# Fewer unread products, a re-searched plan, and the last rows cast in two operations, in a two-layer transformer kernel

## Chip, cores and metric

The kernel runs on one core of one Trainium2 chip. The metric is the device time of one execution in microseconds (us), read as the median of several executions. Nothing but this kernel runs on the core.

## What is computed

Two transformer layers over x of 2048 rows by 448 columns, in bfloat16, with the same weights in both layers. Each layer is a layernorm, attention with 16 heads of 28 columns, and a dense part of 448 to 1792 to 448 columns with a squared ReLU:

```python
x = x + _A_ref(_layernorm(x), A_wqkv, A_wo)         # softmax(q k^T / sqrt(28)) v, then wo
x = x + _B_ref(_layernorm(x), B_w1, B_b1, B_w2, B_b2)   # h = relu(x w1 + b1); (h * h) w2 + b2
x = x + _A_ref(_layernorm(x), A_wqkv, A_wo)
x = x + _B_ref(_layernorm(x), B_w1, B_b1, B_w2, B_b2)
```

The scores are 2 layers x 16 heads x 2048 x 2048, 134 million exponentials. They are the bulk of the work of every engine but SyncE.

## The kernel before

**Units.** A layer's rows are cut into blocks of 256 query rows, and the last 256 rows of layer 1 into two blocks of 128. A pass is one block and one group of four heads. Its work is cut into units of 128 x 512 scores, one bank of PSUM each; there are 2048 units in all. TensorE (PE) makes the scores of a unit with 32-row products (line 1107, `sc<-Q_sb,K_sb`), three units at a time into a tile of three banks, of which there are two (`ps_sc`).

**Exponentials.** ScalarE (ACT) takes the exponential of the two or three banks of a tile in one instruction (line 1139, `pts<-sc`, 1024 or 1536 columns). Some units, here 328 of 2048, are kept from ACT: VectorE (DVE) copies their scores away (line 1211), GpSimd (POOL) and DVE make the exponential out of integer and float arithmetic on the bits (lines 1236, 1242, 1251, 1263), or DVE closes it alone with a longer operation (line 1275). Such a unit has a bank of its own (`mt`) or the third bank of a tile. PE then multiplies by the values (line 1336, `oT<-pts,V_sb`).

**What sets the order.** The program is written out by a planner (`class Planner`). It holds a clock for each engine and a list of streams: the score stream, the exponential stream, the stream of products with values, one stream for each chain of a block (output projection, layernorm, dense part, next layer's q, k and v), and others. At each step it takes the operation that could start first by its own durations and priorities, and writes it. Each engine then runs its instructions strictly in the order written, so the plan decides the order and the hardware's semaphores the times. The streams' choices are steered by tables of 128 numbers, one for each 128th of the units (`step[0]`): `OWN3` (whether a unit for DVE and POOL may take a bank of its own), `PACE` (how much DVE work may be waiting when one is taken), `MIXT` (whether POOL or DVE closes it), `CPRE`, `LASTP`, `STOPS` (priorities and end of these), `BYDMA` (whether a normalised block is transposed by a DMA, line 717, or by PE with a copy on DVE, lines 735 and 747).

**Unread products.** After each group of scores a stream called `heat` (line 1767, `mt<-xn,ident`, 448 columns) looks at the planned share of PE's array in the last 1.8 us, in which a product counts by the part of the array that it fills. Where that share is under `WARM`, it puts in one or two products that nobody reads; `s_stream` repeats a group's score products for the same reason under `WARM2`. `heat` ends 100 units before the last.

**The end.** When the last scores are written, what is left is one chain over the last 128 rows (`finish` and `ends_last`). The output projection and the residual meet in one bank (line 1590). DVE casts these rows to bfloat16 (`rows`, line 1596), takes their moments (`st`, line 1635, `mg`, line 1639), and adds the small constant (line 1651); POOL takes the power -1/2 (line 1657). PE transposes the rows that are not normalised yet, three quarters of the columns at once (line 1611), ACT copies them (line 1618), and PE opens two tiles of the dense part with them (line 1695). The moments are put in as extra columns of the fourth quarter (lines 1661 to 1670, the last two with POOL's result), which is transposed and copied by DVE (line 1620) and closes the tiles. Then come ReLU and square (lines 1708 to 1714), the second product (line 835), and the scaling with the sum of the residual (line 1740), stored by two DMAs (line 1744).

Of the kernel before, what the change touches and what calls it, by code (L numbers as in the profile page):

```python
# [48 lines left out]
WARM = 0.55  # L49
WARM2 = 0.55  # L50
# [25 lines left out]
PRE = 0.5  # L76
# [22 lines left out]
OWN3 = (0.0, 0.0, 0.0, 0.0, 0.0, 0.0, 1.0, 1.0, 0.0, 0.0, 0.0, 0.0, 1.0, 1.0, 1.0, 1.0, 1.0, 1.0, 0.0, 1.0, 0.0, 1.0, 0.0, 0.0, 1.0, 0.0, 1.0, 1.0, 0.0, 0.0, 0.0, 1.0, 0.0, 1.0, 0.0, 0.0, 0.0, 1.0, 0.0, 1.0, 1.0, 0.0, 1.0, 0.0, 0.0, 1.0, 0.0, 0.0, 0.0, 0.0, 0.0, 1.0, 0.0, 0.0, 0.0, 1.0, 0.0, 0.0, 0.0, 0.0, 0.0, 1.0, 1.0, 1.0, 1.0, 0.0, 1.0, 0.0, 0.0, 1.0, 0.0, 0.0, 1.0, 1.0, 1.0, 1.0, 1.0, 1.0, 0.0, 0.0, 0.0, 1.0, 1.0, 1.0, 0.0, 0.0, 1.0, 0.0, 1.0, 0.0, 0.0, 1.0, 0.0, 0.0, 1.0, 1.0, 1.0, 1.0, 0.0, 1.0, 0.0, 0.0, 0.0, 0.0, 1.0, 1.0, 1.0, 1.0, 0.0, 1.0, 0.0, 0.0, 0.0, 0.0, 1.0, 1.0, 1.0, 1.0, 0.0, 0.0, 1.0, 0.0, 0.0, 0.0, 0.0, 0.0, 0.0, 0.0)  # L99
# [12 lines left out]
PACE = (1.4, 3.0, 3.0, 1.4, 3.0, 1.4, 2.2, 4.0, 3.0, 3.4, 3.0, 3.0, 4.0, 4.0, 3.0, 3.0, 4.0, 3.4, 3.4, 3.4, 2.2, 3.0, 3.4, 4.0, 4.0, 3.4, 1.4, 4.0, 2.2, 3.0, 3.0, 4.0, 4.0, 4.0, 3.0, 4.0, 4.0, 3.4, 2.2, 3.0, 3.0, 4.0, 3.0, 4.0, 1.4, 3.0, 3.4, 3.4, 3.0, 3.4, 3.0, 3.0, 3.0, 3.0, 2.2, 4.0, 1.4, 4.0, 2.2, 4.0, 4.0, 4.0, 3.0, 2.2, 2.2, 2.2, 3.0, 3.4, 2.2, 3.0, 4.0, 3.0, 2.2, 2.2, 3.0, 4.0, 1.4, 3.4, 3.4, 3.0, 3.4, 2.2, 3.0, 2.2, 3.0, 4.0, 1.4, 3.4, 3.4, 3.4, 3.4, 3.4, 4.0, 3.0, 4.0, 1.4, 2.2, 4.0, 3.0, 2.2, 3.4, 2.2, 3.4, 3.4, 3.0, 4.0, 3.0, 3.0, 1.4, 4.0, 3.0, 3.0, 3.0, 2.2, 3.0, 2.2, 3.4, 3.4, 3.0, 1.4, 3.0, 3.0, 3.0, 3.0, 3.0, 3.0, 3.0, 3.0)  # L112
MIXT = (1.8, 1.2, 1.2, 1.2, 1.2, 1.8, -9.0, 1.2, 1.2, 1.8, 1.2, 1.2, -9.0, 1.2, -9.0, 1.2, 1.2, 1.8, -9.0, 1.2, 1.2, 1.2, -9.0, -9.0, -9.0, 1.8, 1.2, 1.2, 1.2, 1.2, -9.0, 1.2, 1.8, 1.2, -9.0, -9.0, 1.2, 1.2, 1.2, -9.0, 1.8, 1.2, 1.2, 1.2, 1.2, 1.2, 1.8, 1.2, -9.0, 1.2, 1.2, 1.2, 1.2, 1.2, 1.2, -9.0, 1.2, 1.8, 1.2, 1.2, 1.2, 1.8, -9.0, 1.2, 1.8, 1.2, 1.2, -9.0, 1.8, -9.0, -9.0, -9.0, -9.0, 1.2, 1.8, 1.8, 1.8, 1.2, 1.8, 1.2, 1.2, 1.8, -9.0, 1.8, 1.2, 1.2, -9.0, 1.2, 1.8, 1.8, -9.0, 1.2, 1.8, 1.8, 1.8, 1.2, 1.2, -9.0, 1.2, -9.0, -9.0, -9.0, 1.2, -9.0, 1.2, 1.2, -9.0, 1.8, -9.0, 1.8, 1.2, 1.2, -9.0, 1.2, 1.2, 1.2, 1.8, -9.0, -9.0, 1.8, 1.8, -9.0, 1.2, 1.2, 1.2, 1.2, 1.2, 1.2)
# [9 lines left out]
LASTP = (3.2, 3.2, 3.2, 3.2, 3.2, 3.2, 3.2, 3.2, 3.2, 3.2, 3.2, 3.2, 3.2, 3.2, 3.2, 3.2, 3.2, 3.2, 3.2, 3.2, 3.2, 3.2, 3.2, 3.2, 3.2, 3.2, 3.2, 3.2, 3.2, 3.2, 3.2, 3.2, 3.2, 3.2, 3.2, 3.2, 3.2, 3.2, 3.2, 3.2, 3.2, 3.2, 3.2, 3.2, 3.2, 3.2, 3.2, 3.2, 3.2, 3.2, 3.2, 3.2, 3.2, 3.2, 3.2, 3.2, 3.2, 3.2, 3.2, 3.2, 3.2, 3.2, 3.2, 3.2, 3.2, 3.2, 3.2, 3.2, 3.2, 3.2, 3.2, 3.2, 3.2, 3.2, 2.6, 2.6, 3.2, 3.2, 3.2, 3.2, 3.2, 2.6, 3.2, 3.2, 3.2, 3.2, 4.4, 3.2, 1.5, 2.6, 3.2, 3.2, 3.2, 3.2, 3.2, 2.6, 1.5, 1.5, 2.6, 1.5, 3.2, 1.5, 4.4, 1.5, 3.2, 2.6, 2.6, 3.2, 4.4, 3.2, 3.2, 3.2, 3.2, 3.2, 3.2, 3.2, 4.4, 1.5, 3.2, 3.2, 4.4, 4.4, 3.2, 3.2, 3.2, 3.2, 3.2, 3.2)  # L123
# [260 lines left out]
def kernel(  # L384
# [12 lines left out]
    nc = tc.nc  # L397
# [1177 lines left out]
    def finish(l, qb, ahead_of):  # L1575
# [20 lines left out]
        rows = Op("DVE", 0.61, lambda e: nc.vector.tensor_copy(out=xr[:, 0:D], in_=box["p"]), deps=[last])  # L1596
# [8 lines left out]
        def turn(dcs, deps):  # L1605
            b = {}

            def tr(e):
                b["t"] = bank(t, "tp").bitcast(DT.bfloat16).rearrange("p (c q) -> p c q", c=NDC)
                for dc in dcs:  # L1610
                    nc.tensor.transpose(out=b["t"][:, dc, 0:P], in_=xr[:, dc * P:(dc + 1) * P], identity=ident[:, :])
# [207 lines left out]
```

## Time and profile before

| | |
|---|---|
| median of 3 runs | 806.33 us (805.58 to 806.5) |
| the profiled execution | 805.64 us |
| its span, first to last instruction | 803.9 us |
| ACT busy, share of the span | 788.0 us, 98% |
| POOL busy, share of the span | 472.2 us, 59% |
| DMA: bytes moved, share of 16 engines | 18.56 MB, 10% |

The table is read against one chain: ACT has something to do in nearly all of the span. [...] The span is that of the instructions; the execution's own time is 1.74 us longer.

### The profile page before, as it was taken

To read this page: it belongs to the slowest core of one execution; us is meant where nothing else is said; L and a number is where in the kernel's file an instruction comes from. 1 tells how busy PE (TensorE), PEld (TensorE's weight loads), DVE (VectorE), ACT (ScalarE), POOL (GpSimd) and SP (SyncE) were. 2 spreads that over 40 slices of the span, in tenths; PEclk is the share of its full clock that TensorE was granted. 3 is DMA by queue.
4 is the path that set the end of the run, shared out by engine and by line. 5 is a ranking of instruction groups with operands and counts; after the bars stand their busy time and mean duration, and the time that the engine had idled before them with its cause. 6 is when DMAs were issued, how large, how long until landed. Compare 5 with 4: busy or idle time off the path is not lost.

```text
span 803.9 us, 27471 instructions
## 1 busy us (share of the span) xinstructions
PE 756.9 (94%) x11319; PEld 395.0 (49%) x11319; DVE 763.7 (95%) x1713; ACT 788.0 (98%) x679; POOL 472.2 (59%) x738
## 2 busy tenths in 40 slices
PE   8999999999999999999999999889999999999998
PEld 5544445454545445454554445434454544545665
DVE  7999999999999999999999999999999999999955
ACT  8999999999999999999999999999999999999994
POOL 3264665666666666665566677667666666565500
PEclk9999999999999999999999999999999999999999
DMA  9300000011010110010000000010100001010100
GB/s 245 89 22 9 9 15 10 9 22 22 8 16 10 22 22 9 14 26 20 2 15 2 2 2 3 9 30 16 41 15 14 15 20 28 15 27 9 31 15 13
DMA packets 50862, 18.56 MB, mean 23 GB/s; under 512 B 36585, under 2 KB 50283, under 8 KB 50736
## 3 DMA queue, kind: packets, MB, share of 16 engines
q1 hardware_dynamic: 50736, 16.81, 9.2%
q8 instruction: 88, 1.44, 0.8%
q14 instruction: 38, 0.31, 0.1%
HBM read 10.28 MB, written 1.95 MB: 15 GB/s over the span
## 4 chain that ended last, share of the span: by engine, by line
ACT 36%; PE 28%; DVE 24%; issue 11%; POOL 1%; ACTq 0%; DVEq 0%; POOLq 0%
ACT pts L1139 36%; PE mt L835 12%; PE sc L1107 8%; DVE v_w L1211 5%; PE oT L1336 4%; DVE r L1532 3%; DVE pts L1263 2%; DVE pts L1242 2%; DVE K_sb L1211 2%; DVE st L662 2%; DVE V_sb L1263 1%; DVE V_sb L1242 1%; DVE x_sb L1474 1%; PE sc L835 1%; DVE V_sb L1541 1%
## 5 line engine op out<-in xcount | busy, mean ns | idle before, releaser
L1139 ACT ACTIVATE pts<-sc 128x1536 bf16<-128x1536 f32 (+1 forms) x664 | 777.8, 1352 | 2.0 <-PE sc L1107 1.1
L1107 PE MATMUL sc<-Q_sb,K_sb 32*128 32x256 bf16 (+1 forms) x4344 | 270.4, 265 | 31.6 <-ACT pts L1139 24.7
L1107 PEld LDWEIGHTS <-K_sb 32*128 32x128 bf16 x4468 | 102.9, 92 | 201.1 <-issue 148.8
L1251 POOL TENSOR_SCALAR v_w<-v_w 128x512 int16<-128x512 f32 x224 | 148.2, 661 | 69.3 <-DVE V_sb L1263 9.7
L1336 PE MATMUL oT<-pts,V_sb 128*32 128x256 bf16 (+1 forms) x3986 | 154.3, 268 | 0.4 <-DVE K_sb L747 0.2
L1211 DVE TENSOR_SCALAR v_w<-sc 128x512 f32<-128x512 f32 x203 | 137.5, 681 | 2.8 <-PE sc L1107 2.3
L835 PE MATMUL mt<-xnT,w 128*128 128x256 bf16 (+1 forms) x888 | 116.9, 271 | 4.0 <-DVE r L1532 3.1
L1336 PEld LDWEIGHTS <-V_sb 128*32 128x32 bf16 x4352 | 90.9, 96 | 51.0 <-issue 37.7
L1236 POOL TENSOR_SCALAR V_sb<-v_w 128x512 bf16<-128x512 uint16 x107 | 76.3, 713 | 52.9 <-DVE v_w L1211 16.2
L1236 POOL TENSOR_SCALAR pts<-v_w 128x512 bf16<-128x512 uint16 x109 | 75.1, 689 | 47.2 <-DVE v_w L1211 16.0
L835 PEld LDWEIGHTS <-w 128*128 128x128 bf16 x896 | 76.0, 97 | 37.1 <-issue 28.1
L1532 DVE TENSOR_SCALAR r<-mt 128x512 bf16<-128x512 f32 x108 | 73.8, 683 | 5.5 <-PE mt L835 4.2
L1251 POOL TENSOR_SCALAR K_sb<-K_sb 128x512 int16<-128x512 f32 x90 | 59.2, 657 | 32.3 <-DVE pts L1263 6.9
L835 PE MATMUL mt<-w,V_sb 128*128 128x448 bf16 (+2 forms) x288 | 67.4, 345 | 0.0
L1242 DVE TENSOR_TENSOR pts<-pts 128x512 bf16<-128x512 bf16 (+1 forms) x117 | 61.8, 529 | 0.1
L1242 DVE TENSOR_TENSOR V_sb<-V_sb 128x512 bf16<-128x512 bf16 (+1 forms) x114 | 56.2, 493 | 0.5 <-POOL V_sb L1236 0.5
L1211 DVE TENSOR_SCALAR K_sb<-sc 128x512 f32<-128x512 f32 x69 | 47.0, 682 | 0.8 <-PE sc L1107 0.5
L1263 DVE TENSOR_TENSOR pts<-pts,v_w 128x512 int16<-128x512 bf16 (+1 forms) x93 | 43.2, 465 | 1.0 <-POOL v_w L1251 0.5
L1263 DVE TENSOR_TENSOR V_sb<-V_sb,v_w 128x512 int16<-128x512 bf16 (+1 forms) x93 | 41.3, 445 | 0.8
L1236 POOL TENSOR_SCALAR pts<-K_sb 128x512 bf16<-128x512 uint16 x46 | 30.4, 661 | 17.4 <-DVE V_sb L1541 3.6
L1474 DVE TENSOR_TENSOR x_sb<-x_sb,mt 128x448 bf16<-128x448 bf16 x61 | 37.1, 609 | 3.1 <-PE mt L835 2.4
L662 DVE BATCH_NORM_STATS2 st<-x_sb 128x6 f32<-128x448 bf16 x63 | 38.6, 614 | 0.8 <-DMA x_sb<-in_A_x_dram 0.7
(151 smaller groups left out, 882.8 us busy)
## 6 DMA issues: line engine op xcount, KB each, us to landing
rec<-scr SPq DMA_DIRECT2D x54, 64.0 KB
x_sb<-in_A_x_dram SPq DMA_DIRECT2D x8, 224.0 KB
out_dram<-x_sb SPq DMA_DIRECT2D x15, 112.0 KB
w<-in_B_w_dram SPq DMA_DIRECT2D x1, 1568.0 KB
w<-in_B_w_dram SPq DMA_DIRECT2D x1, 1344.0 KB
dn<-oT_sb SPq DMA_DIRECT2D x54, 2.0 KB
V_sb<-in_A_wqkv_dram SPq DMA_DIRECT2D x4, 168.0 KB
xnT<-xn SPq DMA_TRANSPOSE x34
```

The lines of the kernel that those rows point to most:

```text
L662: return nc.vector.bn_stats(out=box["st"][:, :], in_=x_sb[:, t0 + j, :] if src is None else src())
L835: nc.tensor.matmul(box["t"][:, c0:c0 + n], lhsT=lhsT() if callable(lhsT) else lhsT, rhs=rhs, start=a, stop=b)
L1107: nc.tensor.matmul(dst[k][:, i * nt * P:(i + 1) * nt * P], lhsT=K_sb[l][rows, g, (kb + i) * P:(kb + i + 1) * P], rhs=Q_sb[rows, g, t0 * P: ...
L1139: t = nc.scalar.activation(out=pt[:, 0:n], in_=gbuf[gi]["sc"][:, 0:n], func=AF.Exp, scale=float(np.log(2.0)) * 2.0 ** -FRAC)
L1211: t = nc.vector.tensor_scalar(out=box["w"], in0=two(src), scalar1=EXP_SHIFT, scalar2=EXP_LOW, op0=ALU.add, op1=ALU.max)
L1236: return nc.gpsimd.tensor_scalar(out=two(pd), in0=low, scalar1=-EXP_MID * 65536, scalar2=EXP_BEND, op0=ALU.add, op1=ALU.mult)
L1242: return nc.vector.tensor_tensor(out=pd, in0=pd, in1=pd, op=ALU.mult)
L1251: return nc.gpsimd.tensor_scalar(out=two(box["t"]), in0=box["w"], scalar1=EXP_BITS, scalar2=1.0, op0=ALU.add, op1=ALU.mult)
L1263: return nc.vector.tensor_tensor(out=pd.bitcast(DT.int16), in0=pd, in1=t, op=ALU.add)
L1336: nc.tensor.matmul(box["t"][DHP * hh:DHP * hh + DHP, 0:n], lhsT=V_sb[l][:, kb + i, 4 * g + hh, :], rhs=p[:, c0:c0 + n], start=begin and kb ...
L1474: return nc.vector.tensor_tensor(out=x_sb[:, tb, lo:hi], in0=x_sb[:, tb, lo:hi], in1=t[:, 0:hi - lo], op=ALU.add)
L1532: return nc.vector.tensor_scalar(out=r[:, 0:w], in0=t[:, 0:w], scalar1=0.0, scalar2=None, op0=ALU.max)
```

## The change

1. `WARM` and `WARM2` go from 0.55 to 0.45: unread products are put in only where the planned share of the array is lower than before.
2. The tables `OWN3`, `PACE`, `MIXT`, `LASTP`, `STOPS`, `CPRE` and `BYDMA` have other numbers. The whole order is written anew from them, from the first 50 us on.
3. In `finish`, the last rows are cast in two operations: columns 0 to 255 ahead of the moments, columns 256 to 447 behind the first of their two operations. The first two quarters are transposed as soon as the first half is cast. The third is transposed and copied by itself, and the fourth shares the first two's bank instead of taking one.
4. In `ends_last`, the two tiles of the dense part are opened with the first two quarters, then take the third, then the fourth. The last chain's priority is `ENDP` once no scores are left.

```diff
-WARM = 0.55
-WARM2 = 0.55
+WARM = 0.45
+WARM2 = 0.45
...
-OWN3 = (0.0, 0.0, 0.0, 0.0, 0.0, 0.0, 1.0, 1.0, 0.0, 0.0, 0.0, 0.0, 1.0, 1.0, 1.0, 1.0, 1.0, 1.0, 0.0, 1.0, 0.0, 1.0, 0.0, 0.0, 1.0, 0.0, 1.0, 1.0, 0.0, 0.0, 0.0, 1.0, 0.0, 1.0, 0.0, 0.0, 0.0, 1.0, 0.0, 1.0, 1.0, 0.0, 1.0, 0.0, 0.0, 1.0, 0.0, 0.0, 0.0, 0.0, 0.0, 1.0, 0.0, 0.0, 0.0, 1.0, 0.0, 0.0, 0.0, 0.0, 0.0, 1.0, 1.0, 1.0, 1.0, 0.0, 1.0, 0.0, 0.0, 1.0, 0.0, 0.0, 1.0, 1.0, 1.0, 1.0, 1.0, 1.0, 0.0, 0.0, 0.0, 1.0, 1.0, 1.0, 0.0, 0.0, 1.0, 0.0, 1.0, 0.0, 0.0, 1.0, 0.0, 0.0, 1.0, 1.0, 1.0, 1.0, 0.0, 1.0, 0.0, 0.0, 0.0, 0.0, 1.0, 1.0, 1.0, 1.0, 0.0, 1.0, 0.0, 0.0, 0.0, 0.0, 1.0, 1.0, 1.0, 1.0, 0.0, 0.0, 1.0, 0.0, 0.0, 0.0, 0.0, 0.0, 0.0, 0.0)
+OWN3 = (0.0, 0.0, 0.0, 0.0, 0.0, 1.0, 0.0, 1.0, 0.0, 0.0, 1.0, 0.0, 1.0, 0.0, 1.0, 0.0, 1.0, 1.0, 0.0, 0.0, 0.0, 1.0, 1.0, 0.0, 0.0, 0.0, 0.0, 1.0, 0.0, 1.0, 0.0, 1.0, 0.0, 0.0, 0.0, 0.0, 0.0, 1.0, 0.0, 1.0, 0.0, 0.0, 0.0, 0.0, 0.0, 1.0, 1.0, 1.0, 0.0, 1.0, 0.0, 1.0, 0.0, 0.0, 0.0, 1.0, 0.0, 0.0, 0.0, 0.0, 0.0, 0.0, 1.0, 0.0, 1.0, 1.0, 1.0, 1.0, 0.0, 1.0, 0.0, 1.0, 1.0, 1.0, 1.0, 1.0, 0.0, 0.0, 0.0, 0.0, 1.0, 1.0, 1.0, 1.0, 0.0, 0.0, 1.0, 1.0, 0.0, 0.0, 0.0, 1.0, 1.0, 0.0, 0.0, 1.0, 1.0, 1.0, 0.0, 0.0, 0.0, 0.0, 0.0, 0.0, 0.0, 1.0, 1.0, 1.0, 1.0, 1.0, 1.0, 0.0, 0.0, 0.0, 1.0, 1.0, 1.0, 0.0, 1.0, 0.0, 1.0, 0.0, 0.0, 0.0, 0.0, 0.0, 0.0, 0.0)
...
+ROWS2 = 0
+OPEN1 = 2
+ENDP = 2.6
...
-            pl.spawn((lambda now: LASTP[step[0]]) if (l, qb) == (1, len(blocks[1]) - 1) else lambda now: 4 + 0.1 * qb - (PRE if (l, qb) not in rows_done else 0.0) - CPRE[step[0]], ends_last(l, qb) if (l, qb) == (1, len(blocks[1]) - 1) else chain(l, qb))
+            pl.spawn((lambda now: LASTP[step[0]] if s_left else ENDP) if (l, qb) == (1, len(blocks[1]) - 1) else lambda now: 4 + 0.1 * qb - (PRE if (l, qb) not in rows_done else 0.0) - CPRE[step[0]], ends_last(l, qb) if (l, qb) == (1, len(blocks[1]) - 1) else chain(l, qb))
...
-        rows = Op("DVE", 0.61, lambda e: nc.vector.tensor_copy(out=xr[:, 0:D], in_=box["p"]), deps=[last])
+        cut = 2 * P
+        rows = Op("DVE", 0.41, lambda e: nc.vector.tensor_copy(out=xr[:, 0:cut], in_=box["p"][:, 0:cut]), deps=[last])
...
-        def turn(dcs, deps):
+        def turn(dcs, deps, by=None, within=None):
...
-                b["t"] = bank(t, "tp").bitcast(DT.bfloat16).rearrange("p (c q) -> p c q", c=NDC)
+                b["t"] = box["tp"][1]["t"] if within else bank(t, "tp").bitcast(DT.bfloat16).rearrange("p (c q) -> p c q", c=NDC)
...
-            o = yield from turn([0, 1, 2], [rows])
+            o = yield from turn([0, 1], [rows])
...
-        st = Op("DVE", 0.62, take, deps=[last], rel=first)
+        st = Op("DVE", 0.62, take, deps=[last])
         yield st
+        more_rows = Op("DVE", 0.35, lambda e: nc.vector.tensor_copy(out=xr[:, cut:D], in_=box["p"][:, cut:D]), deps=[last], rel=first)
+
+        def rest_of_rows():
+            yield more_rows
+            o = yield from turn([2], [more_rows], "ACT")
+            pl.tok["rows2"] = o
+        late_rows = rest_of_rows()
+        if ROWS2 == 0:
+            pl.spawn(2.7, late_rows)
...
-        tail = turn([3], [o])
+        tail = turn([3], [o], within=box["tp"][0])
...
-            for i in range(2):
-                yield part_of(i, [0, 1, 2], done)
+            for i in range(OPEN1):
+                yield part_of(i, [0, 1], done)
+            yield Op("-", 0.0, None, deps=["rows2"])
+            for i in range(OPEN1):
+                yield part_of(i, [2], [pl.tok["rows2"]])
...
-        for i in range(2, 4):
-            o = part_of(i, [0, 1, 2, 3], [ev3])
+        for i in range(OPEN1, 4):
+            o = part_of(i, [0, 1, 2, 3], [ev3, pl.tok["rows2"]])
```

**In the order, on DVE at the end.** Before, from the cast of the last rows to the copy of the fourth quarter (`xn_107` holds the rows and the extra columns, `ve` and `rstd` the variance and its root, `x_sb<-x_sb,sc` is the sum of the block before the last one):

```order
L1596 CAST xn_107<-mt 128x448
L1635 BN_STATS st<-mt 128x6
L1639 BN_AGGR mv<-st 128x2
L1651 TENSOR_SCALAR ve<-mv 128x1
L1661 TENSOR_SCALAR xn_107<-mv 128x1
L1662 SCALAR_TENSOR_TENSOR xn_107<-mv,xn_107 128x1
L1663 COPY xn_107<-xn_107 128x1
L1664 CAST xn_107<-ve 128x1
L1665 TENSOR_TENSOR xn_107<-ve,xn_107 128x1
L1474 TENSOR_TENSOR x_sb<-x_sb,sc 128x448
L1669 TENSOR_TENSOR xn_107<-ve,rstd 128x1
L1670 SCALAR_TENSOR_TENSOR xn_107<-ve,rstd,xn_107 128x1
```

The same place of the changed kernel, up to the copy:

```order
L1600 CAST xn_107<-mt 128x256
L1643 BN_STATS st<-mt 128x6
L1650 CAST xn_107<-mt 128x192
L1647 BN_AGGR mv<-st 128x2
...
L1684 TENSOR_TENSOR xn_107<-ve,xn_107 128x1
L1688 TENSOR_TENSOR xn_107<-ve,rstd 128x1
L1689 SCALAR_TENSOR_TENSOR xn_107<-ve,rstd,xn_107 128x1
L1477 TENSOR_TENSOR x_sb<-x_sb,sc 128x448
L1627 COPY xnT<-sc 128x128
```

The cast stands on both sides of the moments' first operation, and the sum of the other block has moved from ahead of the two operations that need POOL's root to behind them, ahead of the fourth quarter's copy.

**On PE at the end.** Before, from the last product of the output projection (`wo,oTn`) on; `sc<-w,V_sb` is the second dense product of the block before, 14 products of which five stand ahead of this place:

```order
L1590 MATMUL mt<-wo,oTn 128x448
...
L835 MATMUL sc<-w_95,V_sb_102 128x448
...
L1611 MATMUL sc<-ident,xn_107 128x128
...
L835 MATMUL sc<-w_95,V_sb_102 128x448
...
L1695 MATMUL mt<-xnT,w_94 128x128
...
L1611 MATMUL sc<-ident,xn_107 128x128
...
L1695 MATMUL mt<-xnT,w_94 128x128
```

The same place of the changed kernel:

```order
L1593 MATMUL mt<-wo,oTn 128x448
...
L838 MATMUL sc<-w_95,V_sb_102 128x448
...
L1615 MATMUL sc<-ident,xn_107 128x128
...
L838 MATMUL sc<-w_95,V_sb_102 128x448
...
L1615 MATMUL tp<-ident,xn_107 128x128
...
L1714 MATMUL mt<-xnT,w_94 128x128
...
L838 MATMUL sc<-w_95,V_sb_102 128x448
...
L1714 MATMUL mt<-xnT,w_94 128x128
```

Before, it was six second products, three transposes, three second products, 24 products that open the two tiles, one transpose and eight that close them. Now it is four second products, two transposes, four second products, one transpose, eight opening products, the last second product, eight more opening products, the fourth quarter's transpose, eight products of the third quarter and eight that close. Ahead of this place, before the last score group's products with values (16 products `oT<-pts,V_sb`), there now stand four products of the output projection that stood 22 products earlier.

**On PE where column sums of a weight are made** (line 539 before, 542 after), in the sixth hundred of microseconds. Before:

```order
L539 MATMUL mt<-wq,w_94 128x128
L1767 LDWEIGHTS ident
L1767 MATMUL mt<-xn_105,ident 128x448
L1767 LDWEIGHTS ident
L1767 MATMUL mt<-xn_105,ident 128x448
L1107 LDWEIGHTS K_sb_100
L1107 MATMUL sc<-Q_sb,K_sb_100 128x256
```

The first such place of the changed kernel:

```order
L542 MATMUL mt<-wq,w_94 128x128
L1110 LDWEIGHTS K_sb_100
L1110 MATMUL sc<-Q_sb,K_sb_100 128x256
```

Two unread products that stood between the sums and the next score group are gone here. Over the whole order their number goes from 85 to 55.

More of the change, by code (lines that the diff above doesn't have):

```diff
@@ L1620, in ev @@
                     return nc.vector.tensor_copy(out=dst, in_=src)
-            o = Op("ACT" if len(dcs) > 1 else "DVE", 0.23 + 0.11 * len(dcs) if len(dcs) > 1 else 0.22, ev, deps=[t], rel=t)
+            by = by or ("ACT" if len(dcs) > 1 else "DVE")
+            o = Op(by, 0.23 + 0.11 * len(dcs) if by == "ACT" else 0.22, ev, deps=[t], rel=within or t)
             b["o"] = o
@@ L1653, in finish @@
         yield ve
+        if ROWS2 == 1:
+            pl.spawn(2.7, late_rows)
         def root(e):
```

21 lines of the change are left out of this document (12 added, 9 removed).

## Prediction

> **What bounds the kernel now.** First the page: busy times, and the granted clock in 40 slices.
>
> ```profile
> PE 756.9 (94%) x11319; PEld 395.0 (49%) x11319; DVE 763.7 (95%) x1713; ACT 788.0 (98%) x679; POOL 472.2 (59%) x738
> PEclk9999999999999999999999999999999999999999
> ```
>
> Three engines are busy for over nine tenths, ACT most, and TensorE has its full clock in every slice. Next the groups of ACT with shapes kept apart, and two rows of its timeline, in which neighbours are merged: a start, a duration, a count.
>
> ```profile
> L1139 ACT ACTIVATE pts<-sc 128x1536 bf16<-128x1536 f32 x392 | 558.5, 1525 | 1.9 <-PE sc L1107 1.1 <-ACT pts L1139 0.4 <-PE mt L1107 0.2
> L1139 ACT ACTIVATE pts<-sc 128x1024 bf16<-128x1024 f32 x272 | 282.2, 1103 | 0.2
> ...
> 11.15 6.82 ACT L1139 ACTIVATE pts<-sc 128x1536 bf16<-128x1536 f32 x5 [0.61 <-PE sc L1107]
> ...
> 768.69 21.65 ACT L1139 ACTIVATE pts<-sc 128x1536 bf16<-128x1536 f32 x16
> ```
>
> A long exponential lasts 1.525 us, but 16 of them fit in 21.65: the step from start to start is (21.65 - 1.525) / 15 = 1.342 us there, and (6.82 - 1.525) / 4 = 1.324 in the first five. So 0.18 to 0.20 of each overlaps the next, and a short one steps by 1.103 less that, 0.902 to 0.920. From the first start, 11.15, to the last end, 790.34, are 779.2 us; 392 long and 272 short steps are 764.4 to 776.3 of it. **ACT's stream is the bound**, with 3 to 15 us of late starts spread through it, most of them too short to show as idle. Before it lie 11.15 us of loading, behind it 13.56 to the end of the span.
>
> Who waits for whom on PE, and the busy time of the middle 600 us (the columns: PE, weight loads, DVE, ACT, POOL, each with its count, then clock and DMA):
>
> ```profile
> PE sc L1107 <- ACT pts L1139: 24.7, 56, 1.1
> ...
> 100.00:700.00 600.00, 565.62 (x8216) 287.49 (x8213) 585.14 (x1284) 599.04 (x518) 386.20 (x597) 1.00 0.07 15
> ```
>
> PE's longest wait is for a score tile that ACT has not yet read, 24.7 us in 56 waits: PE is ahead of ACT far more often than behind it. DVE has 600 - 585.14 = 14.9 us idle in the middle, PE 34.4.
>
> **Unread products and the tables.** Counted in the order, `mt<-xn,ident` goes from 85 to 55 and the repeated score products from 116 to 88.
>
> ```profile
> 771.02 0.93 PE L835 MATMUL mt<-w,V_sb 128*128 128x448 bf16 x4
> ...
> 773.41 1.12 PE L835 MATMUL mt<-w,V_sb 128*128 128x448 bf16 x5
> ...
> 776.38 0.39 PE L735 MATMUL tp<-ident,xn 128*128 128x128 bf16 x4
> ...
> 782.33 0.40 PE L1107 MATMUL sc<-Q_sb,K_sb 32*128 32x128 bf16 x12 [0.28 <-ACT pts L1139]
> ```
>
> A product of 448 columns costs 1.12 - 0.93 = 0.19 us in a row of such, so 30 fewer are 5.7 us of PE; of the repeats a whole group is 0.40 us and six products of 256 columns have the columns of twelve of 128, so 28 are at most 28 / 6 x 0.40 = 1.9 us. Four transposes take at most 0.39, so the 16 more that PE now makes cost at most 1.6. PE is lighter by some 6 us. Nearly all of it lies beside ACT's work, since a faster PE first adds to the 24.7 us of waiting; it is worth something only where an unread product stood ahead of a late score group. Bounds: nothing, and all 6 us. I take it with the tables, below.
>
> ACT still does 1720 units (1176 + 544 before, 1158 + 562 now), in 386 long and 281 short instructions: -6 x 1.342 + 9 x 0.920 = **+0.2 us**, on the path.
>
> DVE and POOL still do 328 units, closed otherwise:
>
> ```profile
> L1263 DVE TENSOR_TENSOR V_sb<-V_sb,v_w 128x512 int16<-128x512 bf16 x86 | 36.5, 425 | 0.7
> ...
> L747 DVE COPY xnT<-tp 128x1024 bf16<-128x1024 bf16 x9 | 6.1, 678 | 0.0
> ...
> L1263 DVE TENSOR_TENSOR V_sb<-V_sb,v_w 128x1024 int16<-128x1024 bf16 x7 | 4.9, 693 | 0.1
> L1275 DVE SCALAR_TENSOR_TENSOR V_sb<-v_w,V_sb 128x512 int16<-128x512 f32 x7 | 4.8, 682 | 0.0
> ```
>
> Closes of 512 columns go from 270 to 249 (-21 x 0.425 = -8.9), of two units at once from 22 to 29 (+7 x 0.693 = +4.9), of DVE alone from 14 to 21 (+7 x 0.682 = +4.8), and four DMA transposes fewer mean two more copies of 1024 columns (+2 x 0.678 = +1.4). DVE gets 2.2 us more. What hides it is DVE's 14.9 us of idle time in the middle; if that cover is gone where the work falls, it costs up to 2.2 us. POOL loses seven operations, and SP four issues; both have room.
>
> What the new order does to ACT's late starts is not in the trace of before. It can close at most the 3 to 15 us that there are; it can also make as many. It leaves 6 us less on PE and 2.2 us more on DVE, and nine more short exponentials, which give PE 0.9 instead of 1.3 us for whatever stands between two score groups. I take **0**, with -2.7 (a third of the middle, 9, less the 0.2) and +2.2 as ends for the range.
>
> **The end.** The timeline, start and duration first:
>
> ```profile
> 784.01 1.08 PE L1336 MATMUL oT<-pts,V_sb 128*32 128x128 bf16 x64
> ...
> 787.71 0.40 PE L1107 MATMUL sc<-Q_sb,K_sb 32*128 32x128 bf16 x12
> ...
> 788.54 0.35 PE L1590 MATMUL mt<-x_sb,ident 128*128 128x448 bf16 x1
> ...
> 788.73 0.73 PE L1590 MATMUL mt<-wo,oTn 128*128 128x448 bf16 x3
> ...
> 789.73 0.51 PE L835 MATMUL sc<-xnT,w 128*128 128x128 bf16 x6
> ...
> 792.50 0.62 DVE L1596 CAST xn<-mt 128x448 bf16<-128x448 f32 x1 [0.46 <-PE mt L1590]
> 793.04 0.62 DVE L1635 BATCH_NORM_STATS2 st<-mt 128x6 f32<-128x448 f32 x1
> ...
> 793.70 0.18 DVE L1639 BATCH_NORM_AGGREGATE mv<-st 128x2 f32<-128x6 f32 x1
> ...
> 793.80 0.48 ACT L1618 COPY xnT<-sc 128x384 bf16<-128x384 bf16 x1 [1.92 <-PE sc L1611]
> ...
> 794.14 0.56 POOL L1657 TENSOR_TENSOR rstd<-ve,mhalf 128x1 f32<-128x1 f32 x1 [18.55 <-DVE xn L1661]
> ...
> 794.51 0.16 DVE L1665 TENSOR_TENSOR xn<-ve,xn 128x1 bf16<-128x1 f32 x1
> 794.58 0.62 DVE L1474 TENSOR_TENSOR x_sb<-x_sb,sc 128x448 bf16<-128x448 bf16 x1
> 795.11 0.16 DVE L1669 TENSOR_TENSOR xn<-ve,rstd 128x1 bf16<-128x1 f32 x1
> 795.30 0.22 DVE L1670 SCALAR_TENSOR_TENSOR xn<-ve,rstd,xn 128x1 bf16<-128x1 f32 x1
> ...
> 795.67 0.22 PE L1611 MATMUL sc<-ident,xn 128*128 128x128 bf16 x1
> ...
> 795.92 0.22 DVE L1620 COPY xnT<-sc 128x128 bf16<-128x128 bf16 x1 [0.40 <-PE sc L1611]
> ...
> 796.20 0.61 PE L1695 MATMUL mt<-xnT,w 128*128 128x128 bf16 x8 [0.32 <-DVE xnT L1620]
> ```
>
> And two casts of scores' size from PSUM, for the halves:
>
> ```profile
> L1363 DVE CAST oT_sb<-oT 128x256 bf16<-128x256 f32 x33 | 13.7, 415 | 0.2
> ...
> L1363 DVE CAST oT_sb<-oT 128x128 bf16<-128x128 f32 x2 | 0.6, 278 | 0.0
> ```
>
> Read as a chain: cast, moments, POOL's root, two small operations, transpose, copy, the closing products. (1) The 448-column cast lets the next operation start 0.54 us on; the 256-column one lasts 0.415, 0.21 less, so the moments start about 0.33 on. (2) The second cast, between 0.28 and 0.415, say 0.35, now stands between the moments' two operations; with the same overlap it frees DVE 0.54 + 0.27 = 0.81 behind the moments' start, where before the second operation came 0.66 behind it. From the cast's start that is 0.33 + 0.81 = 1.14 instead of 1.20: the moments are only 0.06 early. (3) POOL's root ended at 794.70, but DVE was in `x_sb<-x_sb,sc` until 795.11. That sum now stands behind the two operations, so they start when the small operation of 794.51 ends, 794.67, and the root, 794.70, both 0.06 earlier, with 0.05 for the hand-over: 794.69 instead of 795.11, 0.42 earlier. (4) What is late next is the copy: the sum starts some 0.40 after the first of the two, 795.09, and lets DVE go 0.53 on, as before, at 795.62; the transpose, 0.42 earlier, would have allowed 795.50. The copy starts at 795.62 instead of 795.92, and the closing products with it: **-0.3 us**. Bounds of this: -0.42 with the sum wholly hidden, and 0 if the copy waits as long as before.
>
> The third quarter runs beside this: its transpose stands eight second products (8 x 0.19 = 1.5 us) behind the projection's last, which let the cast start at 792.50, so at some 793.9; ACT copies a smaller piece than the three quarters that took 0.48 us, and its eight products stand behind the fourth quarter's transpose, with half a microsecond to spare. Ahead of the last 16 products with values there now stand 48 others (three quarters of 1.08, 0.81), six (0.51) and four of the projection (at most 1.08): 2.4 us with drains, from 788.1 on (the last score group, 787.71 and 0.40), against the last exponential's end at 790.34. So these 16 start at 790.5 at the latest, where they now can start at about 790.4. I put that at 0, with 0.2 as its bound.
>
> Sum for the profiled execution: 805.64 + 0.2 + 0 - 0.3 = 805.5. The median of the three runs, 806.33, is 0.7 above it and their lowest 0.1 below; I add 0.3, half-way, so that the forecast stands for a median: **805.8**. What a measurement of this kernel can tell from no change is about 0.2%, 1.6 us; this lies within.
>
> **The clock.** The change takes work off the array, so the granted clock is the thing to weigh. Three stretches of before in which PE was least loaded, and the first products of the kernel beside later ones of their size:
>
> ```profile
> 85.00:88.40 3.40, 2.45 (x33) 1.00 0.02 1
> 267.30:270.70 3.40, 2.24 (x52) 1.00 0.48 80
> 535.60:539.00 3.40, 2.09 (x48) 1.00 0.13 31
> ...
> L835 PE MATMUL mt<-w,V_sb 128*128 128x448 bf16 x260 | 64.5, 355 | 0.0
> ...
> L498 PE MATMUL mt<-b2w 128*128 128x448 bf16 x11 | 4.3, 578 | 1.3 <-DVE b2w L480 1.3
> ```
>
> With PE busy for 2.1 of 3.4 us the clock stays at 1.00. The eleven products at the very start took 4.3 us, 0.39 each, twice the 0.19 of later ones: that is what slow ones look like. [...]
>
> **The rivals.** (A) *The lighter PE closes late starts.* For it: 30 fewer products in the way. Against it: PE waits for ACT 24.7 us already. Price: -2.7 on the sum: 805.8 - 2.7 = 803.1. (B) *DVE becomes the bound, and the kernel is slower.* Place: the middle 600 us, 97.5% busy. It decides as soon as the 2.2 us more of DVE's work falls where DVE has no idle time left: score copies come late, banks stay occupied, and PE and ACT wait. Price: +2.2, 808.0. Against it: 14.9 us of idle time. (C) *The clock drops* in some stretches of 3.4 us. At half speed 2.1 to 2.45 us of products become 4.2 to 4.9, which loses 0.8 to 1.5 each; three such stretches, +2.4 to +4.5: 808.2 to 810.3. (D) *The end does not do what it says*: the sum only changes places with the copy, and nothing is gained: 806.1, still no change.
>
> **How the numbers follow.** Forecast 0.55, D 0.13, A 0.18, B 0.10, C 0.04. No change is forecast and D: 0.68. Faster by over 0.2% (under 804.7) is A: 0.18; slower (over 807.9) is B and C: 0.14. The range reaches to A and B without taking in all of either: 803.5 to 808.0.
>
> **What would show it.** In the changed profile: ACT's exponentials as 386 and 281, with a first start near 11.15; from the last exponential's end to the span's end 13.3 instead of 13.56; the copy of the fourth quarter directly behind the sum; the granted clock at 1.00 in each slice. DVE's busy time in the middle should rise by about 2 us. Wrong would be a last exponential more than 1.5 us away from 790.5 either way: then the new order's late starts, which I put at no change, decide.

## The result, and the profile after

| | before | after |
|---|---|---|
| median, 8 runs each | 806.18 us (805.58 to 806.55) | 811.61 us (808.95 to 817.79) |
| after / before, 95% interval | | 1.0076 (1.0059 to 1.0092) |
| granted clock | 1.000 in the profiled run, 0.999 or 1.000 in the 35 runs beside the experiments | 0.985 to 1.000, run by run |
| the profiled execution, its span | 805.64, 803.9 | 812.69, 810.8 |

The kernel became slower: 5.4 us between the medians, outside the predicted range. The runs of after also differ among themselves, and in step with the clock: 808.95 and 809.01 us at a clock of 1.000; 809.76 and 810.53 at 0.998; 812.69 at 0.994, 813.46 at 0.994 and 813.89 at 0.993; 817.79 at 0.985. So there are two parts. At full clock the new order is about **2.8 us** slower than before; the rest, **2.6 us** at the median, goes with the clock.

First the page of after: the span, busy times, the granted clock in 40 slices, and the two groups of exponentials.

```profile
span 810.8 us, 27362 instructions
...
PE 757.8 (93%) x11277; PEld 395.2 (49%) x11277; DVE 768.6 (95%) x1710; ACT 790.6 (98%) x683; POOL 468.9 (58%) x731
...
PEclk9999999999999999999999997999999999999999
...
L1142 ACT ACTIVATE pts<-sc 128x1536 bf16<-128x1536 f32 x386 | 550.2, 1517 | 5.2 <-PE sc L1110 4.0 <-PE mt L1110 0.6 <-ACT pts L1142 0.2
L1142 ACT ACTIVATE pts<-sc 128x1024 bf16<-128x1024 f32 x281 | 288.5, 1097 | 1.0 <-PE sc L1110 0.5
```

ACT is still the busiest engine and has 386 and 281 exponentials. What is new is the 7 in the row of the clock, and 4.0 us in which ACT waited for scores ahead of a long exponential, where before had 1.1. The windows of after: the middle, then 3.4 us ahead of the slow place, the slow place, and 3.4 us behind it (PE, weight loads, DVE, ACT, POOL, then clock, DMA share and GB/s).

```profile
100.00:700.00 600.00, 561.33 (x8108) 284.80 (x8107) 584.81 (x1276) 595.20 (x515) 381.58 (x590) 0.99 0.07 14
491.60:495.00 3.40, 2.62 (x41) 1.52 (x41) 3.25 (x8) 3.12 (x4) 2.38 (x5) 1.00 0.04 9
495.00:505.30 10.30, 9.68 (x96) 4.37 (x99) 8.03 (x17) 8.13 (x8) 6.20 (x10) 0.50 0.20 24
505.30:508.70 3.40, 3.24 (x59) 1.44 (x52) 2.56 (x6) 3.23 (x3) 1.57 (x4) 1.00 0.02 5
```

For 10.3 us the clock was at one half, no value between. ACT, busy for 595.20 of the middle 600 us, was busy for 8.13 of these 10.30. Note also what PE's busy time says: 9.68 of 10.30 us, because the same products simply last longer. The timeline of after, from the kernel's first block and then inside that stretch, shows how such products look:

```profile
10.26 1.04 PE L838 MATMUL mt<-xnT,wk 128*128 128x256 bf16 x8
...
498.15 0.93 PE L1789 MATMUL mt<-xn,ident 128*128 128x448 bf16 x2
...
501.85 1.86 PE L838 MATMUL mt<-xnT,wk 128*128 128x256 bf16 x8
...
503.65 1.03 PE L1110 MATMUL sc<-Q_sb,K_sb 32*128 32x256 bf16 x6
...
504.77 1.45 ACT L1142 ACTIVATE pts<-sc 128x1536 bf16<-128x1536 f32 x1 [1.44 <-PE sc L1110]
```

Eight products of 256 columns take 1.86 instead of 1.04 us, stand between two score groups, and the exponential behind them starts 1.44 us late.

**Where the 6.9 us between the two spans lie.** Late starts are counted here as what a step from one exponential's start to the next has over 1.33 us (long) or 0.903 (short), the shortest steady steps of these traces (the prediction had 1.342 and 0.92).

| us | before | after | difference |
|---|---|---|---|
| first exponential starts | 11.15 | 11.66 | +0.5 |
| steps of all exponentials, with no late start (their counts times these steps) | 765.65 | 765.79 | +0.14 |
| late starts from 2 us ahead of the slow stretch to 3.4 us behind it | 0 | 3.3 | +3.3 |
| late starts elsewhere | 11.85 | 15.1 | +3.2 |
| last exponential's end to the span's end | 13.52 | 13.37 | -0.15 |

The first line is no effect of the change: it lies anywhere between 10.8 and 11.7 in the profiled executions of this study. In these two the clock comes up during the loading at 5.8 us (before) and 6.9 us (after), and six products with `b2w` there take 1.59 us in before and 2.11 in after. Of the 3.3 us, 0.45 lie ahead of the drop of the clock and so are no effect of it.

### The profile page after: what moved, and what is told of

It is laid out like the page before. It is cut to its first block, busy times and chain, and to the rows that moved or that the text cites. A ratio compares the mean times of both kernels' runs of the same rounds, so it can differ in the third digit from the quotient of the medians.

```text
span 810.8 us, 27362 instructions
## 1 busy us (share of the span) xinstructions
PE 757.8 (93%) x11277; PEld 395.2 (49%) x11277; DVE 768.6 (95%) x1710; ACT 790.6 (98%) x683; POOL 468.9 (58%) x731
## 3 DMA queue, kind: packets, MB, share of 16 engines
q8 instruction: 88, 1.44, 0.8%
## 4 chain that ended last, share of the span: by engine, by line
PE 34%; ACT 27%; DVE 26%; issue 10%; POOL 2%; ACTq 0%; DVEq 0%; POOLq 0%
ACT pts L1142 27%; PE mt L838 15%; PE sc L1110 10%; PE oT L1339 5%; DVE v_w L1214 5%; DVE r L1535 3%; DVE pts L1266 2%; DVE K_sb L1214 2%; DVE pts L1245 2%; DVE V_sb L1245 1%; DVE st L665 1%; DVE V_sb L1266 1%; DVE x_sb L1477 1%; DVE V_sb L1544 1%; DVE K_sb L861 1%
## 5 line engine op out<-in xcount | busy, mean ns | idle before, releaser
L1110 PE MATMUL sc<-Q_sb,K_sb 32*128 32x256 bf16 (+1 forms) x4340 | 274.9, 267 | 37.6 <-ACT pts L1142 32.9
L1254 POOL TENSOR_SCALAR v_w<-v_w 128x512 int16<-128x512 f32 x217 | 144.3, 665 | 71.5 <-DVE pts L1266 11.6
L1239 POOL TENSOR_SCALAR pts<-v_w 128x512 bf16<-128x512 uint16 x123 | 85.0, 691 | 72.4 <-DVE v_w L1214 21.5
L1239 POOL TENSOR_SCALAR V_sb<-v_w 128x512 bf16<-128x512 uint16 x98 | 68.4, 698 | 42.5 <-DVE v_w L1214 9.3
L1245 DVE TENSOR_TENSOR pts<-pts 128x512 bf16<-128x512 bf16 (+1 forms) x123 | 63.6, 517 | 0.0
L1214 DVE TENSOR_SCALAR K_sb<-sc 128x512 f32<-128x512 f32 x79 | 53.7, 681 | 0.6 <-PE sc L1110 0.4
L1266 DVE TENSOR_TENSOR pts<-pts,v_w 128x512 int16<-128x512 bf16 (+1 forms) x104 | 47.7, 459 | 1.2
L1239 POOL TENSOR_SCALAR pts<-K_sb 128x512 bf16<-128x512 uint16 x39 | 27.8, 712 | 17.0 <-DVE K_sb L1214 4.4
L1266 DVE TENSOR_TENSOR V_sb<-V_sb,v_w 128x512 int16<-128x512 bf16 (+1 forms) x77 | 35.5, 462 | 1.5 <-POOL v_w L1254 0.5
```

The source lines that it names most:

```text
L1110: nc.tensor.matmul(dst[k][:, i * nt * P:(i + 1) * nt * P], lhsT=K_sb[l][rows, g, (kb + i) * P:(kb + i + 1) * P], rhs=Q_sb[rows, g, t0 * P: ...
L1214: t = nc.vector.tensor_scalar(out=box["w"], in0=two(src), scalar1=EXP_SHIFT, scalar2=EXP_LOW, op0=ALU.add, op1=ALU.max)
L1239: return nc.gpsimd.tensor_scalar(out=two(pd), in0=low, scalar1=-EXP_MID * 65536, scalar2=EXP_BEND, op0=ALU.add, op1=ALU.mult)
L1245: return nc.vector.tensor_tensor(out=pd, in0=pd, in1=pd, op=ALU.mult)
L1254: return nc.gpsimd.tensor_scalar(out=two(box["t"]), in0=box["w"], scalar1=EXP_BITS, scalar2=1.0, op0=ALU.add, op1=ALU.mult)
L1266: return nc.vector.tensor_tensor(out=pd.bitcast(DT.int16), in0=pd, in1=t, op=ALU.add)
```

## The experiments

Theories: (T1) the clock: fewer unread products let the array's clock fall in places, and products at half speed bring scores late; (T2) the order: the plan made from the new tables has more late score groups at any clock; (T3) the end costs something. Each ratio is against runs of before on the same chip (medians of 805.5 to 806.1). The unread products change no output.

**e1, before without them.** The order of before, but its 85 products of `heat` are not issued.

```diff
-                    for _ in range(k):
+                    for _ in range(0):
                         nc.tensor.matmul(t[:, 0:D], lhsT=ident[:, :], rhs=xns[0][:, 0:D], start=True, stop=True)
```

> The kernel before in exactly its order on every engine, but the 85 unread products of line 1767 are not issued (the repeated score products stay). Theory clock: what is lost in the changed kernel is array activity, so with still less of it the granted clock falls below 1.00 in this order too, in stretches of 10.24 us at half speed that cost about 3.7 us each; three to ten of them, clock 0.94 to 0.98, 815 to 840 us. Theory order: the unread products only take PE's time, and what slowed the changed kernel is where the new tables put the work; then this kernel keeps the clock at 1.00 and stays at 805 to 806 us, or gains a little from 16 us less work on PE.

Measured: 809.72 us (807.89 to 813.06), ratio 1.0054 (1.0032 to 1.0075), clocks 0.983 to 0.992 where before had 1.000. Less work on PE made the kernel slower; the size expected was far too large. The windows of this kernel, ahead of two slow stretches and in them:

```profile
267.30:270.70 3.40, 2.00 (x44) 0.88 (x44) 3.40 (x9) 3.40 (x4) 2.01 (x3) 1.00 0.58 84
270.70:274.10 3.40, 3.24 (x20) 0.99 (x19) 2.33 (x6) 2.40 (x3) 1.89 (x3) 0.50 0.26 42
523.30:526.70 3.40, 1.77 (x32) 0.93 (x30) 3.40 (x10) 3.40 (x4) 1.94 (x4) 1.00 0.04 1
526.70:533.50 6.80, 6.22 (x86) 2.97 (x79) 5.48 (x14) 6.36 (x6) 4.12 (x6) 0.50 0.11 28
```

In 3.4 us of the slow clock ACT lost 1.0 us. On the 632 exponentials that lie well outside the slow stretches this kernel has 10.9 us of late starts, before 11.7: without slow clock it would have gained some 0.8. So an unread product costs a little where it stands in the way, and T1 holds: it pays by the clock.

**e2, after with each of its 55 issued twice** (`range(2 * k)`).

> The changed kernel in exactly its order, but each of its 55 unread products is issued twice. Theory clock: the activity comes back in the places where the plan found it low, so the clock stays at 1.00 in all or nearly all executions and the time falls from 811.6 to about 809, the value of those executions of the changed kernel that had a clock of 1.000, with a spread under 1 us. Theory order: 10 us more work on PE changes nothing or makes it slower, 811 to 814, and the spread of the executions stays.

Measured: 816.13 us (814.88 to 820.38), 1.0135 (1.0105 to 1.0165), clocks 0.992, 1.000, 1.000, 0.998. The time that T1 expected was missed: even the two runs at a clock of 1.000 took 815 us, since the doubled products stand ahead of late score groups (20.9 us of late starts outside slow stretches). And the clock was not cured (two of four runs at 1.000, in after two of eight): doubling adds nothing in places where none stands.

**e3 and e4, the end alone.** e3 is before with parts 3 and 4 of the change only; e4 is after with these parts undone.

```diff
-        rows = Op("DVE", 0.61, lambda e: nc.vector.tensor_copy(out=xr[:, 0:D], in_=box["p"]), deps=[last])
+        cut = 2 * P
+        rows = Op("DVE", 0.41, lambda e: nc.vector.tensor_copy(out=xr[:, 0:cut], in_=box["p"][:, 0:cut]), deps=[last])
...
-            o = yield from turn([0, 1, 2], [rows])
+            o = yield from turn([0, 1], [rows])
```

> The kernel before in its order up to the last scores, with the changed end (the cast in two operations, the third quarter apart, the last chain's priority). Theory end: the copy of the fourth quarter comes 0.38 us earlier against the cast's start and the cast 0.2 us later against the last exponential, so 0.1 to 0.3 us less than before, 805.9 to 806.1, the span behind the last exponential 13.2 to 13.4 instead of 13.5. Rival: the end costs time in an undisturbed kernel, 806.5 or more. In neither case does it explain a part of the 5 us.

> The kernel before with the tables and both thresholds of the change, and the old end. Theories clock and order: as the changed kernel, 809 to 818 with the clock between 0.985 and 1.000 and a median of about 811.8. If the end were what went wrong: 806.

Measured: e3 805.55 us (805.11 to 806.27), 0.9994 (0.9985 to 1.0003), clock 1.000 in all ten runs, late starts 11.85 as before, and 13.11 us from the last exponential's end to the span's end instead of 13.52. e4 811.83 us (810.3 to 816.14), 1.009 (1.0058 to 1.0123), 13.77 instead of after's 13.37. T3 falls: both ways the end gains 0.4 us in the profile (e3's median by itself is not told from no change). On the 656 exponentials outside slow stretches, e4 has 15.15 us of late starts and after 15.08: they belong to the order, not to a run.

**e5 and e6, thresholds and tables apart.** e5 is before with `WARM` and `WARM2` at 0.45; e6 is after with both at 0.55.

```diff
-WARM = 0.45
-WARM2 = 0.45
+WARM = 0.55
+WARM2 = 0.55
```

> The kernel before with only both thresholds at 0.45, planned anew from its old tables (60 unread products instead of 85), old end. Theory clock: the threshold alone brings executions with a clock under 1.00 and a spread of several us. Rival: it needs the new tables too, and here the clock stays at 1.00. Theory order is silent on the clock; since these tables were not made for this threshold, it expects late starts of ACT of 12 to 18 us outside of slow stretches, 806 to 812 us.

> The changed kernel (new tables, new end) with both thresholds back at 0.55: 114 unread products. Theory clock: the clock is 1.000 in all executions, spread under 1.5 us. Theory order: the 3 us that remained of the loss at a clock of 1.000 are in where the work stands, so about 808 to 812 here, without a slow stretch in the trace. Rival: the threshold was all of the loss, 805.5 to 806.5.

Measured: e5 830.46 us (828.97 to 833.69), 1.0312 (1.0283 to 1.0341), with 60 unread products; e6 839.17 (837.97 to 840.52), 1.0415 (1.04 to 1.0431), with 114. The clocks were 0.990 to 0.994 in e5 and 0.990 to 0.992 in e6, where T1 had 1.000 for e6. Both times were missed by 20 to 30 us, and neither theory had the likely reason: changing one threshold moves every later choice of the planner, and the tables fit only the plan they were made for. The diff shown is that of e6. The timeline of e6 where layer 0 ends:

```profile
507.73 2.41 ACT L1142 ACTIVATE pts<-sc 128x1536 bf16<-128x1536 f32 x2
...
510.08 0.62 DVE L1477 TENSOR_TENSOR x_sb<-x_sb,mt 128x448 bf16<-128x448 bf16 x1 [0.51 <-PE mt L838]
...
513.93 0.69 POOL L693 TENSOR_TENSOR rstd<-ve,mhalf 128x2 f32<-128x2 f32 x1
514.65 0.70 DVE L802 TENSOR_SCALAR xn<-x_sb,mv,rstd 128x448 bf16<-128x448 bf16 x2 [1.56 <-POOL rstd L693]
515.12 2.50 SPq L720 DMA_TRANSPOSE xnT<-xn  x2
...
518.89 1.87 PE L838 MATMUL mt<-xnT,wk 128*128 128x256 bf16 x8 [8.08 <-DMA xnT<-xn]
...
522.18 0.98 PE L1110 MATMUL sc<-Q_sb,K_sb 32*128 32x256 bf16 x12
...
522.90 1.94 ACT L1142 ACTIVATE pts<-sc 128x1024 bf16<-128x1024 f32 x2 [12.76 <-PE sc L1110]
```

No scores are left of layer 0, and layer 1's wait for its last keys: residual, moments, root, normalisation and a transpose by DMA follow one another while PE is idle for 8.1 us, and ACT waits 12.8. It is one chain that the plan finished in time with its own tables and late with others. e5 has the same stall at the same place (one wait of 8.0 us). The longer slow stretch in the trace of e6, 10.2 us from 512.7 on, covers most of this stall. So these two say nothing on the clock of the changed order; they say that the threshold's own effect can't be had by undoing the threshold.

**e7 and e8, the same order, place against number.** e7 is e3 with 49 of its 85 unread products, those near stretches of 3.4 us where the other products fill under 0.42 of the array; e8 keeps the other 36. (Share: a product's columns at 0.19 us for 448, times the part of the 128 x 128 array that it uses, summed over the stretch and divided by its length; 3.4 us is what e1's slow stretch from 270.7 lasted. In the comparisons below, a product at an edge counts by the part of its time that lies inside; a count by starts differs by up to 0.09 in the rows compared.)

```diff
+    unread = [0]
...
-                    for _ in range(k):
+                    unread[0] += k
+                    for _ in [i for i in range(unread[0] - k, unread[0]) if i in KEPT]:
```

> The kernel before with the new end, in exactly its order, but of its 85 unread products only the 49 are issued that stand in or near a stretch of 3.4 us in which the other products would fill less than 0.42 of the array. Theory clock (what counts is where they stand): clock 1.000, time as e3_before_new_end or up to 0.7 us less, 804.8 to 805.6. Theory number (what counts is how many there are): the changed kernel has 55 and loses its clock, so 49 lose it too, 808 to 812.

> As e7_unread_where_low, but the other 36 are issued and the 49 left out. Theory clock: those stretches stay low, so the clock falls as in e1_before_no_unread, 0.98 to 0.992, 807.5 to 812.5 us. Theory number: between e1_before_no_unread and e3_before_new_end, clock 0.993 to 1.000.

Measured: e7 805.36 us (804.83 to 805.98), 0.9995 (0.9986 to 1.0005), clock 1.000 in all ten runs; e8 811.8 (810.73 to 813.72), 1.0078 (1.0061 to 1.0095), clocks 0.981 to 0.987. The windows of e8:

```profile
524.90:528.40 3.50, 1.86 (x35) 1.13 (x38) 3.50 (x11) 3.50 (x5) 1.97 (x4) 0.99 0.04 1
528.40:535.20 6.80, 6.23 (x79) 2.74 (x72) 5.42 (x14) 6.52 (x7) 4.45 (x7) 0.50 0.11 28
671.70:675.10 3.40, 1.93 (x36) 0.85 (x35) 3.17 (x6) 3.40 (x4) 2.60 (x4) 1.00 0.36 78
675.10:682.00 6.90, 6.05 (x40) 1.91 (x43) 3.89 (x10) 4.80 (x5) 2.74 (x5) 0.51 0.11 23
```

And the same windows of e7:

```profile
524.90:528.40 3.50, 2.88 (x52) 1.24 (x51) 3.50 (x9) 3.50 (x5) 2.12 (x4) 1.00 0.08 13
528.40:535.20 6.80, 6.37 (x94) 2.97 (x89) 6.06 (x16) 6.80 (x7) 5.06 (x7) 1.00 0.12 22
671.70:675.10 3.40, 2.45 (x26) 0.92 (x24) 3.40 (x9) 3.40 (x4) 1.79 (x3) 1.00 0.14 24
675.10:682.00 6.90, 6.46 (x114) 2.90 (x113) 6.28 (x13) 6.90 (x8) 4.67 (x8) 1.00 0.08 21
```

e7 does the work of these windows 1.7 and 3.0 us earlier than e8, which has been delayed before; there too its clock is 1.00. Six and three unread products more around two places, and the clock stays; without them ACT lost 0.28 us in the one slow stretch and 2.1 in the other. Which products are kept decides, and not the number alone: with 36 kept, e8's clock (0.981 to 0.987) is no better than that of e1 with none (0.983 to 0.992). e7 has the fewest of all kernels that kept their clock, and is the fastest measured, though its interval takes in no difference from before.

**e9 and e10, the changed order with the clock held.** Every instruction of after in its place, and 58 unread products more, each ahead of one score group and into the group's own tile, which the scores overwrite. e9: groups in stretches with a share under 0.40; e10: groups elsewhere.

```diff
+                if gi in ADDED:
+                    nc.tensor.matmul(dst[0][:, 0:D], lhsT=ident[:, :], rhs=xns[0][:, 0:D], start=True, stop=True)
                 for i in list(range(4)) * (again + 1):
```

> The changed kernel, every instruction in its place, and 58 more unread products of 448 columns, each ahead of a score group (in the group's own tile, which the scores then overwrite), in the groups that lie in stretches of 3.4 us where the changed kernel's products fill under 0.40 of the array. If the clock is only part of the loss and the new order's own late starts are the rest: clock 1.000 in all runs, 808.5 to 810 us, that is 3 to 4 us over before, late starts outside slow stretches 15 to 16 us. If the clock were all of it: 805.5 to 806.5. If more products stand in the way as the doubled ones did: over 812 at a clock of 1.000.

> The same with the 58 products ahead of score groups elsewhere, at least seven groups away from any of those. If the place keeps the clock and not the number: clocks of 0.985 to 1.000 from run to run as in the changed kernel, 810 to 814 us. If the number keeps it: clock 1.000 in all runs, and a time like that of the kernel with the 58 in the low stretches.

Measured: e9 814.76 us (814.4 to 815.12), 1.0111 (1.0096 to 1.0126), clock 1.000 in all four runs; e10 816.11 (815.52 to 822.64), 1.0153 (1.0108 to 1.0197), clocks 1.000, 0.983, 1.000, 1.000. The third expectation for e9 came true: the clock holds, and each product ahead of a score group costs about 0.1 us (58 for 5.8 us over the 809.0 of after at full clock). From e9's groups, and then its row of the clock:

```profile
L1105 PE MATMUL sc<-xn,ident 128*128 128x448 bf16 x58 | 20.5, 353 | 7.7 <-ACT pts L1145 7.1 <-DVE h L1269 0.2
...
PEclk9999999999999999999999999999999999999999
```

They stand on the path: 7.1 us of waiting for ACT's tile now lie ahead of them and no longer ahead of the scores. So e9 does not show what the changed order would give with a free cure; that number comes from after's own runs at 1.000. With products in the low stretches four of four runs were at 1.000, where after had two of eight. e10's expectation was half met: three runs kept the clock and one lost it, so by their runs alone e9 and e10 do not tell place from number.

**e11, the changed order without its 55** (`range(0)` again).

> The changed kernel with its 55 unread products not issued and nothing else moved. Before without its 85 had 10.9 us of late starts outside slow stretches, 0.9 less than with them. If the new order's late starts come from the order of what is read: 14 us or more remain outside slow stretches, clock 0.98 to 0.99, 812 to 816 us. If they come from where the 55 stand: 11 to 12 us, and 807 to 811 us at the same clock.

Measured: 817.98 us (817.09 to 823.0), 1.0164 (1.0132 to 1.0195), clocks 0.973 to 0.983: slower than either expectation, at a lower clock. From its page, the row of the clock:

```profile
PEclk9999979999999999999999998899999998899999
```

On the 612 exponentials outside the slow stretches of both, it has 12.4 us of late starts and after 13.2. Without any unread product 12.4 of 13.2 remain: most of T2's late starts come from the order of what is read. Unread products in the way are worth at most 0.8 us here (0.2 if less is left out around the slow stretches), as some 0.8 in e1.

How low the array was filled parts these kernels by their clock. The second and third columns are of the profiled execution of each, between the loading and the end; the last has all runs of the kernel:

| | lowest share in any 3.4 us outside slow stretches | us at half clock | clocks of its runs |
|---|---|---|---|
| before | 0.38 | 0 | 0.999 or 1.000 in the 35 beside the experiments |
| e3, e7 | 0.38, 0.37 | 0 | 1.000 in ten of ten each |
| e9 | 0.41 | 0 | 1.000 in four of four |
| e10 | 0.31 | 0 | 1.000 in three of four, 0.983 |
| after | 0.30 | 10.2 | 0.985 to 1.000 |
| e4 | 0.30 | 3.4 | 0.987 to 0.998 |
| e2 | 0.30 | 13.7 | 0.992 to 1.000 |
| e1, e8 | 0.18, 0.18 | 23.9, 27.3 | 0.983 to 0.992, 0.981 to 0.987 |
| e11 | 0.24 | 44.4 | 0.973 to 0.983 |

The kernels of the table with no 3.4 us under 0.37 kept their clock in every run; those with a lowest share of 0.31 or less lost it in some runs or in all. The share does not tell which place loses it, nor in which run. After has six places at 0.37 or less (the lowest 3.4 us of each start at 110.7, 491.0, 547.0, 678.5, 702.6 and 734.6 us, with 0.35, 0.36, 0.35, 0.32, 0.37 and 0.30), and in this execution the half clock followed the second alone, while two of the eight runs of after had a clock of 1.000. What parts one low place from another, and one run from another, no run shows. The shares are read from one trace of each kernel; no run was made to test them.

## Why the prediction was wrong, point by point

**What bounds it: right.** ACT's stream still sets the time, 98% busy; apart from the first start, all that was lost was lost as late starts of exponentials. Its +0.2 us for three more of them comes to +0.14 with the steps used here. The sign of being wrong that it named is there: the last exponential ended at 797.45, not within 1.5 us of 790.5.

**The step that failed first: rival C at a chance of 0.04.** C was weighed by three rows of before with PE busy 2.09 to 2.45 of 3.4 us at a clock of 1.00. PE's busy time was the poorer quantity to read here: the row of after ahead of its slow stretch has PE busy 2.62, more than these, and the clock fell to 0.50. A score product fills a quarter of the array and counts as fully busy. By share the three rows of before are at 0.45, 0.39 and 0.45, after's at 0.37, and those of e1 ahead of its drops at 0.35 and 0.18: the lowest of before stood little above after's all along, kept there by products of the kind that the change removes (0.39 from 267.3 in before, 0.35 in e1), and the prediction weighed these as work to be saved (6 us of PE, taken as 0). Idle time did not tell either: it was 0.8 of the 3.4 us ahead of after's drop, and 1.3 in the row of before with 2.09 busy that kept its clock. Nor does a low share by itself: the 3.4 us of after from 734.6 have 0.30 and kept a clock of 1.00. C's price per stretch, 0.8 to 1.5 us, was right (1.0 in the row of e1); the number of stretches differs from run to run: at the median 2.6 us.

**The second: the new order's late starts, taken as 0, with +2.2 as their end.** They are +3.2 us, beyond the bound. Of the starts that are over 0.05 us late, 65 in before and 79 in after outside the slow stretch, most (55 and 73) come within 0.15 us of the end of their scores: the scores were late. What stood on PE between the previous score group and the late one, counted in each place with no more than the late start itself: products with values 1.1 us in before and 2.8 in after, dense and other products of the chains 8.3 and 10.0, PE waiting for DVE 1.1 and 2.5, unread products 1.2 and 1.7. These overlap, so each is a bound and not a part of a sum. Fewer unread products closed none of the late starts (rival A, nothing), and most of the rise stands at products written ahead of scores that ACT needed. Why the plan puts them there more often, whether by the tables or by PE time that it believes free, stays open: e5 and e6 were to part the two and could not.

**DVE, rival B: small, its part open.** DVE's time over the whole kernel rose by 4.9 us (768.6 against 763.7) where 2.2 were forecast. The middle 600 us have 584.81, before 585.14, but hold a little less of the work (515 instructions of ACT instead of 518), so they don't tell. From 15 to 790 us PE waits for DVE for 13.3 us in both kernels; by the bounds above, at most 1.5 us more of such waits than before can lie behind late starts.

**The end: right, and cancelled in part.** The timeline of after, from the last 16 products with values to the fourth quarter's copy:

```profile
790.55 6.90 ACT L1142 ACTIVATE pts<-sc 128x1536 bf16<-128x1536 f32 x5
...
797.02 0.73 PE L1593 MATMUL mt<-wo,oTn 128*128 128x448 bf16 x3
797.68 0.41 PE L1339 MATMUL oT<-pts,V_sb 128*32 128x128 bf16 x16
...
799.80 0.42 DVE L1600 CAST xn<-mt 128x256 bf16<-128x256 f32 x1 [0.46 <-PE mt L1593]
800.14 0.62 DVE L1643 BATCH_NORM_STATS2 st<-mt 128x6 f32<-128x448 f32 x1
...
802.31 0.61 DVE L1477 TENSOR_TENSOR x_sb<-x_sb,sc 128x448 bf16<-128x448 bf16 x1
802.84 0.22 DVE L1627 COPY xnT<-sc 128x128 bf16<-128x128 bf16 x1
```

From cast to copy are 3.04 us, before 3.42 (795.92 - 792.50): -0.38 where -0.30 was forecast, and the copy stands right behind the sum, as forecast. But the last exponential ends at 797.45 and the 16 products start at 797.68, behind the three of the projection: from that end to the cast 2.35 us, before 2.16. This +0.19 had been put at 0 with 0.2 as its bound. e3, which keeps before's order ahead of them, has the whole gain: -0.41.

## What to carry to other kernels

A filler product is judged by the place, not by the count: before removing one, ask how full the array is in any 3.4 us around it, by the area that each product fills and not by PE's busy time alone, and read the granted clock of several runs. In the kernels above that kept their clock in every run the lowest such share was 0.37 to 0.41, in those that lost it 0.18 to 0.31. Removing 36 here that no low stretch needed cost nothing; removing the wrong 49 cost 6 us. And here tables fitted to one plan ran 3 to 4% slower with another threshold, so that the threshold could not be changed, nor undone, by itself.

## What the runs showed of the hardware that was not expected

- The half clock lasted 3.4, 6.8 or 10.2 us where it is shown here: 3.4 from 270.7 and 6.8 from 526.7 in e1, 6.8 from 528.4 in e8, 10.2 from 495.0 in after. In after it costs about 0.36 us for each us at half clock, an estimate from its runs: from the one at 0.985 to those at 1.000 are 8.8 us, for 0.015 x 2 x 810 = 24 us at half clock.
- Whether half clock follows a low stretch changes from run to run with the same instructions (after: 0.985 to 1.000 in eight runs), and from place to place in one execution: the 3.4 us of after from 491.6 had a share of 0.37 with PE busy 2.62 us and were followed by a clock of 0.50, those from 734.6 had 0.30 with PE busy 2.13 and kept 1.00. What else counts was not settled.
- Idle time on PE need not be long for it: in the 3.4 us ahead of after's drop PE was idle for 0.8 us in all, and no gap there was over 0.62 us.
